# A rewritten order of work for a long convolution and a token MLP on one core: the same instructions, other queues' sequences

## The chip, the core and the metric

The program runs on one NeuronCore of a Trainium2 chip. The core has five engines with instruction queues of their own: PE (matrix multiply), ACT (ScalarE), DVE (VectorE), POOL (GpSimd) and SP, which here only issues DMA copies. Each queue runs in order. The metric is the device time of one execution in microseconds. The kernel before takes 170.63 us (median of three runs, 170.56 to 170.69).

## What is computed

Inputs are bf16; S = 2048 rows, D = 448 columns, F = 1792.

```python
def _A_ref(q, k, v, shift_k, ssm_k, ssm_D):      # q is already layer-normalized
    # k_shift: causal 4-tap convolution of k along S, one filter per column
    kv = k_shift * v
    # y: causal convolution of kv with ssm_k along S (2048 taps), by FFT of length 4096
    y = irfft(rfft(kv_pad) * rfft(kf_pad))[:S].astype(bf16)
    y = y + kv * ssm_D
    return q * y
def _B_ref(x, w1, b1, w2, b2):                   # x is already layer-normalized
    h = _layernorm(x)
    u = gelu(einsum("bsd,sf->bdf", h, w1) + b1)  # mixes the rows
    return (einsum("bdf,fs->bds", u, w2) + b2).transpose(0, 2, 1)
h  = x + _A_ref(_layernorm(x), ...)
h2 = h + _B_ref(_layernorm(h), ...)
```

## The kernel before

**How the work is staged.** Row s of a tensor lies in partition s // 16, at place s % 16; so one partition holds 16 rows. The long convolution is a transform in two stages of matmuls with sine tables, a product in the frequency domain, and two inverse stages. The code names its steps "tag.n:k": the n-th step of a tag, its k-th operation. The tags are:

- `loads`, `xload`: copies from memory: ssm_k (loads.0 to 3), shift_k (loads.4), k (loads.5, 6, 8, 10 for its slices 3, 0, 1, 2), v (loads.7, 9, 11, 12 for its slices 0, 1, 2, 3), ssm_D, the biases, and x in four slices (xload.0 to 3).
- `tables`: the sine tables and masks. `tables.5` and `tables.6` make the first-stage table E on DVE (integer phases, L837 to L844) and ACT (sine, L847). `tables.4` writes 16 small constants with GpSimd (L820, L821) and decodes the partition number on DVE, ending with a cast (L831, tables.4:20). `tables.7` makes the second-stage tables: three products on GpSimd that read the cast (L854), a sum (L858), a mask and two equality tests on DVE (L860, L866), a sine on ACT (L862) and three products and one negation on GpSimd (L871, L874).
- `kT`: transposes of ssm_k on PE (L1037) and their copies out of PSUM. `kv.1` to `kv.8`: transposes of k (L965). `kv.9` to `kv.16`: the 4-tap convolution as matmuls (L991); DVE multiplies the result with v (L1006).
- `k1`, `u1`: first stage for ssm_k and for k*v, 16 steps each (L1058), a copy out of PSUM (L1066, L1068), and after every second step three DMA copies (two from GpSimd's queue, one from SP's; L1074) that shuffle partitions.
- `k2`, `u2`: second stage (L1093) and copies out of PSUM (L738 to L742).
- `i1`: 16 products on DVE (L1160) in eight pairs, first inverse stage (L1177), copies out of PSUM, and DMA copies into TZ on SP's and GpSimd's queues (L1201; the last pair's, i1.16, L1188). Some of SP's copies fill only the last two of TZ's 16 rows.
- `ct0`, `ct`: transposes of E for the last stage (L1107). `ew`: small tables. `q`, `xn`: statistics of x on DVE (L1237, L1239) and GpSimd (L1245, L1248), and x normalized for four rows (L1270, L1272).
- `i2`: second inverse stage, one row of 16 per step (L1303, L1309), gate with q, layer norm of h; its last step writes a row of Q (L1388).
- `mlp.0` to `mlp.15`: the first MLP matmul for the first seven of 14 blocks of F, one row r each (L1435, W1A); `mlp.17` to `mlp.23`: the other seven blocks (L1445, W1B), with gelu on ACT (L1425); `mlp.24` to `mlp.39`: the second MLP matmul (L1457), the last sum on DVE (L1460) and the copies to the output. `w1a`, `w1b`, `w2`: the weights' copies (L1408, L1412, L1419). `warm`, `dummy`: matmuls whose result is not used. `bias`: a transpose of b1 and a cast of b2.

**What sets the order.** Nothing at run time. `ORDER` holds, for each engine, the whole sequence of its operations; `SLOTS` gives each PSUM tile its bank (eight banks; a tile of two banks takes a pair) and each shuffle buffer its place in a ring of four. The scheduler walks through these lists, checks dependences and emits each engine's instructions in the listed order, with the semaphore waits that the dependences need. So an operation that waits holds up whatever is listed behind it on its engine, and a DMA copy is issued when its queue's engine gets to it. Which of ACT and DVE empties a PSUM tile is also set by which list names it. Two dependences matter outside the data flow: the first product (i1.0) needs every shuffle copy of k1 and u1 to have landed, because its buffers lie in the same memory; and `w1a.1` to `w1a.3`, `w1b` wait for all of i1.16's copies:

```python
op(WQ, lambda e, W, rs=rs: e.dma_start(W1A[:, rs, :], w1d[:, rs, 0:896]),
   w=[(o_W1A + 4 * h * 1792, 4 * 1792)], dmab=128 * 4 * 1792,
   after=shuf["zl"] if h else shuf["u"], safter=(wl[0],) if h else ())
```

## Time and profile before

| | |
|---|---|
| median of three runs | 170.63 us |
| the profiled execution | 170.65 us, of it 168.8 us from the first to the last instruction |
| busy: PE, DVE, ACT, POOL | 160.0, 101.9, 90.4, 58.4 us |
| first product (L1160) starts, last ends | 49.91, 68.86 us |
| PE's first step that waits for i1.16's copies | 75.58 us |
| second MLP matmul | 123.86 to 165.94 us |

A line of the profile names the source line, the engine, the operation and the shapes. "Busy" adds up instructions; for PE the ends of matmuls are modelled, so a busy PE may still be waiting. "Idle before" is the time an engine stood still ahead of an instruction, with what ended it. The chain follows the work that ended last back through what released it. In a timeline the first number is the start, the second the length of a merged piece.

### The profile page before, as it was taken

To read this page: it belongs to the slowest core of one execution; us is meant where nothing else is said; L and a number is where in the kernel's file an instruction comes from. 1 tells how busy PE (TensorE), PEld (TensorE's weight loads), DVE (VectorE), ACT (ScalarE), POOL (GpSimd) and SP (SyncE) were. 2 spreads that over 40 slices of the span, in tenths; PEclk is the share of its full clock that TensorE was granted. 3 is DMA by queue.
4 is the path that set the end of the run, shared out by engine and by line. 5 is a ranking of instruction groups with operands and counts; after the bars stand their busy time and mean duration, and the time that the engine had idled before them with its cause. 6 is when DMAs were issued, how large, how long until landed. Compare 5 with 4: busy or idle time off the path is not lost.

```text
span 168.8 us, 3562 instructions
## 1 busy us (share of the span) xinstructions
PE 160.0 (95%) x1416; PEld 93.3 (55%) x1416; DVE 101.9 (60%) x191; ACT 90.4 (54%) x130; POOL 58.4 (35%) x155
## 2 busy tenths in 40 slices
PE   6999999989899989879999999999999999999994
PEld 2787755453333333334554555555577777777783
DVE  7988999999999999999987440000003213132231
ACT  3599848979999999999685803103550000000000
POOL 8345727694830555675777330000000000000000
DMA  5999898893758766748999999930000111101111
GB/s 161 407 308 385 270 290 327 329 362 126 222 134 318 248 195 186 208 135 273 388 398 403 424 420 422 415 129 0 0 0 9 50 54 54 54 2 56 54 54 54
DMA packets 15564, 35.15 MB, mean 208 GB/s; under 512 B 3804, under 2 KB 9644, under 8 KB 15548
## 3 DMA queue, kind: packets, MB, share of 16 engines
q1 hardware_dynamic: 12396, 28.26, 46.1%
q0 software_dynamic: 3008, 6.58, 12.1%
q8 instruction: 11, 0.18, 0.5%
q10 hardware_dynamic: 144, 0.08, 0.2%
q14 instruction: 5, 0.04, 0.1%
HBM read 22.05 MB, written 1.84 MB: 141 GB/s over the span
## 4 chain that ended last, share of the span: by engine, by line
PE 70%; ACT 14%; DMA 5%; DVE 5%; issue 2%; POOL 2%; SPq 0%; DVEq 0%; ACTq 0%
PE ps L1457 25%; PE ps L1435 13%; PE ps L1445 13%; ACT arena L738 7%; DMA arena<-arena 5%; ACT arena L739 4%; PE ps L1309 3%; PE ps L965 3%; ACT arena L1068 3%; PE ps L1024 3%; PE ps L1058 3%; PE ps L1037 3%; DVE arena L1160 2%; POOL arena L1074 2%; PE ps L991 2%
## 5 line engine op out<-in xcount | busy, mean ns | idle before, releaser
L1460 DVE SCALAR_TENSOR_TENSOR arena<-ps,arena 128x448 bf16<-128x448 f32 (+2 forms) x17 | 11.1, 656 | 55.8 <-PE ps L1457 55.8
L1457 PE MATMUL ps<-arena 128*128 128x448 bf16 (+2 forms) x238 | 42.7, 342 | 0.0
L1457 PEld LDWEIGHTS ps<-arena 128*128 128x128 bf16 x238 | 33.3, 145 | 9.5
L1435 PE MATMUL ps<-arena 128*128 128x448 bf16 x112 | 23.5, 353 | 0.0
L738 ACT CAST arena<-ps 128x896 bf16<-128x896 f32 (+1 forms) x29 | 23.1, 933 | 0.0
L1068 ACT CAST arena<-ps 128x896 bf16<-128x896 f32 x24 | 20.2, 919 | 4.1 <-PE ps L1058 3.6
L1445 PE MATMUL ps<-arena 128*128 128x448 bf16 x112 | 22.3, 352 | 0.0
L1074 POOL DMA_DIRECT2D arena<-arena x32 | 17.6, 556 | 7.9 <-ACT arena L1068 7.7
L1425 ACT ACTIVATE arena<-ps,arena 128x448 bf16<-128x448 f32 x14 | 8.2, 632 | 19.3 <-PE ps L1445 10.3
L1093 PE MATMUL ps<-arena 128*64 128x448 bf16 x128 | 15.3, 361 | 1.8 <-ACT arena L739 0.9
L1435 PEld LDWEIGHTS ps<-arena 128*128 128x128 bf16 x112 | 10.7, 98 | 10.6 <-DVE arena L1388 1.1
L1445 PEld LDWEIGHTS ps<-arena 128*128 128x128 bf16 x112 | 11.0, 98 | 10.2
L1160 DVE TENSOR_TENSOR arena<-arena 128x1792 bf16<-128x1792 bf16 x16 | 16.5, 1083 | 0.0
L1177 PE MATMUL ps<-arena 64*128 64x448 bf16 x128 | 14.1, 351 | 1.1 <-ACT arena L738 0.5
L1058 PE MATMUL ps<-arena 128*32 128x448 bf16 x256 | 14.5, 355 | 0.5 <-ACT arena L1068 0.3
L1201 POOL DMA_DIRECT2D arena<-arena x16 | 9.3, 585 | 13.9 <-ACT arena L738 13.0
L1093 PEld LDWEIGHTS ps<-arena 128*64 128x64 f16 x128 | 5.5, 108 | 10.7 <-ACT arena L739 3.4
L1177 PEld LDWEIGHTS ps<-arena 64*128 64x128 f16 x128 | 5.2, 94 | 9.8 <-DVE arena L1160 3.1
L1388 DVE TENSOR_SCALAR arena<-arena 128x448 bf16<-128x448 f32 x16 | 7.6, 509 | 4.8 <-POOL arena L1381 4.8
L1058 PEld LDWEIGHTS ps<-arena 128*32 128x32 f16 x256 | 5.2, 95 | 7.7 <-ACT arena L1068 2.6
L1237 DVE BATCH_NORM_STATS2 arena<-arena 128x6 f32<-128x448 bf16 x16 | 9.4, 613 | 0.0
L739 ACT ACTIVATE arena<-ps 128x896 bf16<-128x896 f32 x10 | 8.6, 926 | 1.1 <-PE ps L1093 1.1
(99 smaller groups left out, 190.4 us busy)
## 6 DMA issues: line engine op xcount, KB each, us to landing
arena<-in_B_w_dram SPq DMA_DIRECT2D x8, 896.0 KB, 9.9
arena<-in_B_w_dram SPq DMA_DIRECT2D x2, 2048.0 KB, 17.3
arena<-arena SPq DMA_DIRECT2D x16, 224.0 KB, 3.8
arena<-arena POOLq DMA_DIRECT2D x32, 112.0 KB, 3.6
arena<-in_B_w_dram SPq DMA_DIRECT2D x2, 1536.0 KB, 18.8
arena<-arena POOLq DMA_DIRECT2D x13, 196.0 KB, 3.8
arena<-in_A_k_dram SPq DMA_DIRECT2D x4, 448.0 KB, 5.8
arena<-in_A_v_dram SPq DMA_DIRECT2D x4, 448.0 KB, 9.2
```

Of the source, the lines that this page charges most:

```text
L738: return e.copy(out=dst(), in_=src())
L739: return e.activation(out=dst(), in_=src(), func=ACT.Copy, scale=scale)
L1058: op("pe", lambda e, W, b=b, r=r, q=q, x=x, c0=c0: e.matmul(PS[32 * q:32 * q + 32, b.slots[x], 0:D], E[:, 2 * r + x, c0:c0 + 32], src[:, r ...
L1068: return e.copy(out=dst, in_=Ppair(b)) if W == "act" else e.tensor_copy(out=dst, in_=Ppair(b))
L1074: shuf[tag].append(op(q_, lambda e, W, g=g, i=i, a=a, nu=nu, jh=jh: e.dma_start(T[a + i:a + i + 4 * nu - 3:4].rearrange("p (j k) c d -> p ...
L1093: op("pe", lambda e, W, b=bs[h], h=h, j=j, c=c, par=par: e.matmul(PS[64 * par:64 * par + 64, b.slots[c], 0:D], FW[:, 64 * c:64 * c + 64], ...
L1160: op("dve", lambda e, W, m=m, i=i: e.tensor_tensor(out=MR(m.slots[0]).rearrange("p (x y) d -> p x y d", x=2), in0=TU[:, i].unsqueeze(2).br ...
L1177: k = op("pe", lambda e, W, b=bs[h], m=ms[h], par=par, t=t, tab=tab, xy=xy, P=P: e.matmul(Pb(b, par), tab[P, :], MR(m.slots[0])[P, xy, :], ...
L1435: op("pe", lambda e, W, r=r, fc=fc, b=bs[fc]: e.matmul(Pb(b), W1A[:, r, 128 * fc:128 * fc + 128], Q[:, r, :], start=(r == 0), stop=(r == R ...
L1445: op("pe", lambda e, W, r=r, fc=fc, b=b: e.matmul(Pb(b), W1B[:, r, 128 * (fc - n0):128 * (fc - n0) + 128], Q[:, r, :], start=(r == 0), sto ...
L1457: op("pe", lambda e, W, r=r, fc=fc, b=b, d0=d0, d1=d1: e.matmul(Pb(b)[:, d0:d1], W2[fc // 7][:, fc % 7, r:S:R], G[:, fc, d0:d1], start=(fc ...
L1460: op("dve", lambda e, W, r=r, b=b, A=A, d0=d0, d1=d1: e.scalar_tensor_tensor(out=XR(r)[:, d0:d1], in0=Pb(b)[:, d0:d1], scalar=bm[:, r:r + ...
```

## The change

`ORDER` and `SLOTS` are written anew; every operation of before is there after it, none is added or taken away. On PE 1416 operations, on ACT 115, on DVE 177, on GpSimd 151 and on SP 79 stand in both. Thirteen PSUM copies, the small copy of bias.0 and one gate go from ACT to DVE and twelve copies, two gates and one normalization (xn.1) from DVE to ACT. The main moves:

- SP: ssm_k's slice 2 and k's slices 1 and 0 come first; xload.0 and xload.1 stand among the loads, ahead of v's; w1a.0 stands behind i1.16's copies; nine of the copies for TZ's last two rows (i1.1, 8, 10, 12, 14, 6) stand behind w1a.1, w1a.2 and w1a.3.
- GpSimd: the iotas for E come first; the constants of tables.4 are spread over the loads and the first stage; tables.7 stands among the shuffle copies of k1 and u1, and k1.1's first copy behind it.
- DVE: E's phases come first, tables.4:16 to 20 and tables.7 stand among the first-stage copies.
- ACT: E's sines come first, tables.7:5 behind u1.11.
- PE: kT.5 first, the 4-tap convolutions earlier between k1 and u1, ct0.0 behind u1.11, bias.0 behind i1.4, ct.0 behind i2.10, both warm-up matmuls ahead of i2.9; the MLP's matmuls are interleaved over rows and blocks.

The diff, cut ("-" before, "+" after):

```diff
 "pe":
-"dummy.0:1-9 kv.4:0-11 kv.3:0-7 kv.6:0-11 kv.5:0-7 kT.1:0-7 kT.0:0-3 kT.1:9-11 kT.0:4-7 kT.3:0-7 "
-"kT.2:0-3 kT.3:9-11 kT.5:0-7 kT.2:4-7 ct0.0:0-7 kT.6:0-7 kT.7:0-7 bias.0:0 kv.7:0-7 k1.8:0-7 k1.9:0-7 "
...
-"warm.0:0 i2.1:0-3 ct.1:0-7 i2.9:0-3 i2.2:0-1 i2.10:0-1 ct.2:0-7 i2.45:0-1 i2.17:0-1 i2.41:0-1 i2.20:0-1 "
-"i2.54:0-1 i2.28:0-1 i2.32:0-1 warm.1:0 mlp.0:2-6 i2.58:0-1 mlp.0:0-1 mlp.1:0-6 i2.67:0-1 mlp.2:0-6 "
...
+"dummy.0:1-9 kT.5:0-7 kv.6:0-11 kv.5:0-7 kT.4:0-7 kv.4:0-11 kv.3:0-7 kT.0:0-7 kT.1:0-7 kT.3:0-7 kT.1:9-11 "
+"kT.3:9-11 kT.6:0-7 kT.7:0-7 kv.2:0-11 kv.1:0-7 kv.7:0-7 k1.8:0-7 k1.10:0-7 k1.12:0-7 k1.9:0-7 kv.9:0-27 "
...
+"i1.16:10-17 i1.16:1-8 ct.2:0-7 ct.1:0-7 warm.0:0 warm.1:0 i2.9:0-3 i2.1:0-3 i2.2:0-1 i2.10:0-1 ct.0:0-7 "
+"i2.17:0-1 i2.45:0-1 i2.20:0-1 i2.32:0-1 i2.28:0-1 i2.54:0-1 i2.41:0-1 mlp.0:1 mlp.0:5 mlp.0:0 mlp.0:6 "
+"i2.58:0-1 mlp.1:1 mlp.1:5 mlp.0:2-3 mlp.1:2 mlp.1:0 mlp.0:4 mlp.1:4 i2.67:0-1 mlp.1:3 mlp.1:6 mlp.2:4 "
...
 "act":
-"tables.0:5 kv.4:12 kv.3:8 kv.6:12 tables.5:3 tables.6:3 ct0.0:8 bias.0:1 tables.7:5 k1.8:8 k1.9:8 "
...
+"tables.0:5 tables.5:3 kv.5:8 tables.6:3 kv.6:12 kT.3:8 kv.2:12 k1.8:8 k1.12:8 k1.10:8 k1.11:8 k1.13:8 "
+"kT.2:8 k1.14:8 k1.15:8 u1.0:8 u1.1:8 u1.2:8 k1.4:8 u1.3:8 k1.5:8 k1.6:8 k1.7:8 u1.4:8 u1.5:8 u1.8:8 u1.7:8 "
+"u1.10:8 u1.11:8 tables.7:5 u1.13:8 u1.14:8 k2.5:4 k2.1:4 u1.15:8 k2.9:4 k2.13:5 k2.7:4 k2.3:5 u2.13:4 "
...
 "dve":
-"dummy.0:0 tables.3:0-1 kv.0:3 tables.6:0 tables.4:16 tables.5:0 tables.4:17 tables.6:1 tables.4:18 "
-"tables.5:1 tables.4:19 tables.6:2 tables.4:20 tables.5:2 kT.1:8 tables.7:6 kT.0:8 kT.3:8 tables.7:4 "
...
-"q.3:3 u2.13:5 q.3:0 u2.1:5 i1.0:0 i1.1:0 i1.13:0 i1.14:0 i1.9:0 i1.7:0 i1.8:0 i1.10:0 i1.12:0 i1.11:0 "
-"i1.10:18 q.4:3 xn.0:1 i1.5:0 i1.6:0 i1.3:0 i1.6:9 xn.3:1 i1.2:0 i1.16:0 q.4:1 q.3:1 i1.15:0 q.6:0 q.6:2 "
...
+"dummy.0:0 tables.6:0 tables.3:0 tables.5:0 tables.6:1 tables.5:1 kv.0:3 tables.5:2 kT.5:8 tables.6:2 kT.4:8 "
+"tables.3:1 kT.0:8 kT.1:8 kv.3:8 kv.4:12 kT.6:8 kT.7:8 kv.0:4 kv.1:8 kv.7:8 q.1:2 k1.9:8 q.1:0 kv.9:29 "
+"kv.9:28 kv.13:28-29 kv.10:24-25 kv.12:25 kv.12:24 k1.0:8 kv.8:12 k1.1:8 kv.16:24 q.2:0 q.1:1 kv.16:25 q.2:2 "
+"kv.15:29 q.2:3 kv.15:28 tables.4:16-17 kv.11:29 kv.11:28 q.1:3 q.2:1 tables.4:18-19 kv.14:24 tables.4:20 "
+"kv.14:25 k1.2:8 u1.6:8 tables.7:6 u1.9:8 k1.3:8 tables.7:4 ct0.0:8 u1.12:8 q.4:2 q.3:0 k2.5:5 k2.1:5 "
+"tables.7:7 k2.9:5 k2.13:4 k2.7:5 k2.3:4 u2.13:5 u2.1:5 q.3:1 i1.0:0 k2.15:5 i1.14:0 i1.1:0 i1.13:0 i1.7:0 "
+"i1.9:0 i1.10:0 u2.11:5 i1.8:0 i1.12:0 i1.11:0 q.4:3 u2.5:5 q.6:2 i1.6:0 i1.5:0 xn.0:1 xn.3:1 i1.8:18 i1.3:0 "
+"i1.2:0 q.6:3 q.3:2 q.4:0 i1.16:0 i1.15:0 q.5:0 q.3:3 q.8:2 q.4:1 q.6:0 bias.0:1 q.6:1 q.5:1-2 q.7:0 q.5:3 "
...
 "pool":
-"tables.4:0 tables.4:2 tables.4:4 tables.4:6 tables.4:8 tables.4:10 tables.4:12 tables.4:14 tables.4:1 "
...
-"tables.2:7 tables.2:8 tables.2:9 tables.2:10 tables.2:11 tables.2:2 tables.2:4 tables.2:6 q.0:0 q.0:1 "
-"kv.0:1 kv.0:2 tables.7:0 tables.7:1 tables.7:2 tables.7:3 tables.7:8 tables.7:9 tables.7:10 tables.7:11 "
-"kv.0:0 k1.9:9 k1.9:10 k1.11:9 k1.11:10 k1.13:9 k1.13:10 k1.15:9 k1.15:10 u1.1:9 u1.1:10 k1.1:9 k1.1:10 "
...
+"tables.0:1-4 tables.0:0 tables.4:14 kv.0:2 kv.0:1 tables.4:13 tables.1:0 tables.4:12 tables.4:3 tables.4:1 "
...
+"tables.2:10 tables.4:9 k1.9:10 k1.11:10 k1.9:9 k1.15:9-10 k1.13:10 k1.1:10 tables.4:0 k1.13:9 u1.1:9 "
+"tables.2:0 u1.1:10 tables.4:6 tables.4:8 u1.3:10 u1.3:9 k1.5:9-10 q.0:0 tables.7:1-2 k1.7:10 k1.7:9 "
+"tables.7:0 tables.2:9 q.2:4 k1.1:9 tables.7:3 u1.9:9 k1.3:10 tables.7:8 k1.3:9 q.2:5 u1.13:10 u1.13:9 "
+"u1.5:10 u1.5:9 u1.9:10 u1.7:9 tables.7:9 u1.11:10 tables.7:10 u1.7:10 u1.15:9-10 u1.11:9 tables.7:11 ew.0:0 "
...
 "sp":
-"loads.6:0 loads.8:0 loads.0:0 loads.1:0 loads.2:0 loads.3:0 loads.13:1 loads.14:0 loads.14:1 loads.10:0 "
-"loads.5:0 loads.11:0 loads.4:0 loads.4:1 loads.4:2 loads.12:0 loads.9:0 loads.7:0 k1.9:11 k1.11:11 "
-"k1.13:11 k1.15:11 xload.0:0 xload.1:0 u1.1:11 k1.1:11 u1.3:11 k1.5:11 u1.5:11 k1.7:11 u1.7:11 u1.9:11 "
-"k1.3:11 u1.13:11 u1.11:11 u1.15:11 ct0.1:0 ct0.1:1 xload.2:0 xload.3:0 w1a.0:0 ct0.1:2 ct0.1:4 ct0.1:3 "
...
-"i1.4:18 i1.16:19 i1.16:20 w1a.1:0 w1a.2:0 w1a.3:0 w1b.0:0 w1b.0:1 w1b.0:2 w1b.0:3 w2.0:0 w2.0:1 w2.0:2 "
...
+"loads.2:0 loads.8:0 loads.6:0 loads.0:0 loads.1:0 loads.3:0 loads.4:2 loads.4:1 loads.5:0 loads.4:0 "
+"loads.10:0 xload.0:0 loads.11:0 loads.7:0 loads.12:0 loads.13:1 xload.1:0 loads.14:1 loads.9:0 k1.13:11 "
...
+"i1.10:22 i1.4:18 i1.16:19-20 w1a.0:0 w1a.1:0 i1.8:22 i1.8:20 w1a.2:0 i1.10:20 i1.1:20 i1.1:22 i1.12:22 "
+"i1.12:20 i1.14:20 w1a.3:0 i1.6:22 w1b.0:0-3 w2.0:0-3 mlp.25:15 mlp.27:15 mlp.29:15 mlp.31:15 mlp.33:15 "
...
```

`SLOTS` changes with it: the same tiles take other banks of the same eight.

136 rows, old and new, of tables (ORDER, SLOTS) are left out of this document.

## Prediction

> **What bounds the kernel now.** I read the page's totals and slices first, then the chain that ended last, then one table of the engines stage by stage, and only then single instructions.
>
> ```profile
> PE 160.0 (95%) x1416; PEld 93.3 (55%) x1416; DVE 101.9 (60%) x191; ACT 90.4 (54%) x130; POOL 58.4 (35%) x155
> ```
>
> PE at 95% would say that only matmul work counts. The table by stage (start:end, length, then busy time and count for PE, PEld, DVE, ACT, POOL, clock, DMA share, GB/s) says otherwise for the first half:
>
> ```profile
> 24.00:50.00 26.00, 23.84 (x372) 10.60 (x364) 25.22 (x39) 24.00 (x30) 16.79 (x34) 1.00 0.72 256
> 50.00:69.00 19.00, 17.68 (x160) 6.29 (x160) 18.75 (x24) 19.00 (x25) 7.60 (x13) 1.00 0.74 232
> 69.00:75.60 6.60, 5.10 (x46) 2.74 (x47) 6.25 (x17) 6.51 (x9) 5.29 (x9) 1.00 0.56 167
> 75.60:124.00 48.40, 48.40 (x255) 24.74 (x256) 19.23 (x57) 24.00 (x53) 14.91 (x39) 1.00 0.73 285
> ```
>
> From 24 to 69 us DVE is filled to 97% and 99%, ACT to 92% and 100%: they empty PSUM and make the products, and PE, busy by a model of its ends, waits for them. From 75.6 us PE is full (48.40 of 48.40). The chain, in order of time (start, length, what), joins the two:
>
> ```profile
> 67.89 0.99 DVE arena L1160
> 68.92 0.95 PE ps L1177 x8
> 69.89 0.91 ACT arena L738
> 70.82 0.67 SPq L1188
> 71.55 3.99 DMA arena<-arena
> 75.58 2.82 PE ps L1309 x14
> 123.86 42.08 PE ps L1457 x231
> ```
>
> So: the last of the 16 products on DVE (step i1.15) ends at 68.86; 6.7 us later its result has passed PE, ACT and a DMA copy, and the second half starts. That half has 90.4 us of PE work (75.58 to 165.94) without a gap. The change keeps every instruction, so it can gain only by an earlier last product, and lose by a later one or by a hole in the second half. The profiled execution took 170.65 us (span 168.8 and 1.85 around it) beside a median of 170.63, so I carry sums against either.
>
> How much idle time can DVE still give up before that last product? A table of DVE alone between its first instruction and 68.86:
>
> ```profile
> 0.89:68.86 67.97, 65.22 (x102) 1.00 0.81 269
> ```
>
> 2.75 us in all. That is the whole purse for a reordering that leaves DVE's work as it is.
>
> **The change part by part.** DVE's work ahead of the last product is not left as it is. Thirteen PSUM copies come to DVE and twelve go to ACT. In come ten of 128x896 (k1.9, u1.6, u1.9, k2.3, k2.5, k2.9, k2.15, u2.5, u2.11, i1.8) and three of 1024 (kv.3, kv.4, ct0.0), out go eight and four; one more statistics instruction (q.6) stands ahead of the product, one aggregate and a bias cast fewer. Prices, back to back (starts overlap by about 0.08 us):
>
> ```profile
> 43.44 3.10 DVE L742 TENSOR_SCALAR arena<-ps 128x896 bf16<-128x896 f32 x3
> 9.79 1.29 DVE L741 COPY arena<-ps 128x1024 bf16<-128x1024 bf16 x2 [0.19 <-PE ps L1037]
> 33.17 1.14 DVE L1237 BATCH_NORM_STATS2 arena<-arena 128x6 f32<-128x448 bf16 x2
> 49.91 10.22 DVE L1160 TENSOR_TENSOR arena<-arena 128x1792 bf16<-128x1792 bf16 x10
> ```
>
> That is 1.03, 0.64, 0.57 and 1.02 us. 2 x 1.03 - 0.64 + 0.57 - 0.17 = +1.8 us of DVE work. ACT's work to its last copy (i1.16) stays within 0.2 us. So DVE becomes the tighter of the two.
>
> Where it falls matters. Ahead of the first product (i1.0, at 49.91 before) the new order has 1.8 us less DVE work by the same prices: k2.15's second copy and two statistics now stand behind it. From the first product to the end of the last the old order takes 68.86 - 49.91 = 18.95 us; the new one puts four copies there (k2.15, u2.11, u2.5, i1.8) where two were (i1.10, i1.6), and three statistics (q.6, q.3, q.4) where none was: 2.06 + 1.7 - 0.1 = +3.65, so 22.6 us.
>
> Idle time on DVE before the first product, old, is 2.75 less about 0.25 behind it: 2.5 us. New, by place:
> - First instruction. GpSimd makes the two iotas that the first table product (L837) reads ahead of most memsets, so it can start near 1.7 instead of 2.2; DVE is idle 0.35 where it was 0.23.
>
> ```profile
> 1.55 0.34 DVE L810 TENSOR_SCALAR arena<-arena 128x128 bf16<-128x128 int32 x1 [0.23 <-POOL arena L789]
> 2.22 1.23 DVE L837 TENSOR_TENSOR arena<-arena 128x1024 int32<-128x1024 int32 x1
> ```
>
> - ssm_k chunk 2 is loaded first, chunk 0 fourth. DVE reaches kT.0's copy at about 9.2, PE has it transposed at about 9.8: 0.6; kT.6 and kT.7 some 0.4, k1.9 0.1.
> - Loads of x. Two xload slices of 448 KB move ahead of v's slices on SP's queue. The old v loads land up to 9.9 us after their issue at 9.8, so the last at 19.7; 0.92 MB at the 299 GB/s of the first 14 us put 3 us ahead of the last v slice, to about 22.5, and 1.2 us ahead of v's slice 0. DVE wants them at 17.9 (kv.9) and 21.4 (kv.12): a wait between 0 and 2; I take 0.6, since it arrives within a us of both.
> - Later evacuations (k1.1, kv.16) 0.3.
>
> ```profile
> 0.00:14.00 14.00, 12.63 (x132) 9.19 (x135) 12.29 (x26) 9.54 (x10) 7.22 (x47) 1.00 0.89 299
> L901 SPq DMA_DIRECT2D arena<-in_A_v_dram x4: 432/479/586, 6.4 to 9.8; - x4
> DMA to landing us min/median/max: 8.6/9.2/9.9
> ```
>
> - The tables, moved deep into the stretch. GpSimd's three table multiplications (L854) wait for a cast on DVE (L831). In the new order 27.5 us of DVE work stand between 1.7 us and that cast (six integer table steps, eleven transposed copies, fifteen products of L1006, and others by the rows shown), and some 2 us of idle: about 31.4. GpSimd is in order, so behind that wait stand the copies of k1.7, k1.1, u1.9, k1.3, u1.13, u1.5, u1.7, u1.11, u1.15. From the cast to the last copy's issue: 17 DMA issues of 0.54 (9.2), seven table instructions (2 x 0.36, 0.36, 1.0, 3 x 0.43), 1.1 of small ones: 13.7, so 45.1; it lands 2.4 to 3.7 later, 47.5 to 48.8. The first product needs all these copies (its buffers lie in theirs) and DVE gets to it at 48.1 or later: a wait between 0 and 0.7, I take 0.4. PE's first k2 step also waits for k1.1's copy (lands about 38) and for the FW table; PE, DVE and ACT have u1 copies to do until then.
>
> ```profile
> L1006 DVE TENSOR_TENSOR arena<-ps,arena 128x512 bf16<-128x512 f32 x12 | 7.7, 684 | 0.1
> L854 POOL TENSOR_SCALAR arena<-arena x3: 363/364/1331, 7.4 to 9.1; 128x128 int32<-128x128 int32 x3
> L1074 POOL DMA_DIRECT2D arena<-arena x32: 544/544/811, 16.6 to 45.5; - x32
> DMA to landing us min/median/max: 2.4/3.7/5.5
> 43.85 2.15 POOL L1074 DMA_DIRECT2D arena<-arena  x4 [0.36 <-ACT arena L1068]
> 9.53 1.02 POOL L858 TENSOR_TENSOR arena<-arena 128x384 int32<-128x384 int32 x1
> 14.29 1.29 POOL L871 TENSOR_TENSOR arena<-arena 128x128 f16<-128x128 f32 x3 [3.74 <-ACT arena L862]
> ```
>
> Together 2.75 us of idle instead of 2.5: +0.25. So the first product starts at 49.91 - 1.8 + 0.25 = 48.4, the last ends at 48.4 + 22.6 = 71.0, 2.1 us later than 68.86.
>
> Moved at no cost on PE: ct0.0's, ct.0's and bias.0's transposes (0.6 us for eight) lie where PE waits anyway. ct.0 now stands behind i2.10, so its copy on ACT must end before i2.45: in the old run i2.2 ran 2.4 us ahead of the copies' landing (73.21 against 75.58), enough for 0.6 of PE and 0.9 of ACT; without that cover it costs 0.9. A warm-up matmul moves ahead of the copies' landing; PE then waits those 0.2 us for the first normalized row (about 2.9 us behind the landing in both orders), so nothing.
>
> First weights (w1a.0) move from 50.2 us to just behind i1.16's copies. They are wanted 2.9 us behind the copies' landing; a slice took 4.7 us at the least, and this one is issued 3.3 before the landing (75.58 against 72.3), so it lands 1.4 behind it: hidden. Behind w1a.1, which waits for the landing, now queue nine small copies of TZ's last rows at 0.67 us on SP, 6.0 us with the 1.4 of the weight issues: SP gets through at 7.5 us behind the landing, the last copy lands 3.9 later (11.4). PE wants row 14 after 12 steps of i2 (0.38) and 40 matmuls of the MLP (0.19): 12.2. Covered by 0.8; were a landing 6.5, it would cost 1.8. I take 0.
>
> ```profile
> 73.21 0.92 PE L1309 MATMUL ps<-arena 128*128 128x448 bf16 x4 [0.22 <-issue]
> 73.96 0.61 PE L1107 MATMUL ps<-arena 128*128 128x128 f16 x8
> 75.58 2.82 PE L1309 MATMUL ps<-arena 128*128 128x448 bf16 x14 [1.01 <-DMA arena<-arena]
> 78.48 0.74 PE L1435 MATMUL ps<-arena 128*128 128x448 bf16 x3
> L1408 SPq DMA_DIRECT2D arena<-in_B_w_dram x4: 378/440/2027, 50.2 to 76.9; - x4
> DMA to landing us min/median/max: 4.7/7.1/8.6
> L1201 SPq DMA_DIRECT2D arena<-arena x12: 666/666/683, 55.1 to 69.1; - x12
> DMA to landing us min/median/max: 3.3/3.9/6.5
> ```
>
> The interleaved MLP order has the same matmuls in a stretch that is full already: 0. Sum: +2.1, so 172.8 us.
>
> **The rivals.**
> *Faster: DVE never waits.* The place is DVE ahead of the first product. With its 2.5 us of idle all gone, that product starts at 49.91 - 1.8 - 2.5 = 45.6 and the last ends at 68.2: -0.65, 170.0 us. For it: the sine tables come first on ACT, and ACT's 2.3 us wait at 21 to 23 us goes. Against: GpSimd's copies must land by 45.6 too, and the purse is all there is. It decides below 45.9 (0.34 us gained).
>
> ```profile
> ACT arena L1068 <- PE ps L1058: 3.6, 6, 2.3
> ```
>
> *No change:* first product at 45.9 to 46.6, 1.9 to 2.6 us of idle gone, 170.6.
> *Row 14 comes late:* with the last copies' landing at the slow end, 1.3 us more: 174.1. For it: weights fill the same queue; against: 0.8 us of cover.
> *GpSimd's tables stretch.* One L854 took 1331 ns and the two after it 363. The long one lay beside this DVE instruction, and ended with it:
>
> ```profile
> 7.20 1.23 DVE L844 TENSOR_SCALAR arena<-arena 128x2048 int32<-128x2048 int32 x1
> ```
>
> If each of the three took 1.33, the copies behind them would come 2.9 later and the first product at about 50.9: 175.2 us. In the new order PSUM copies run beside them instead, as beside the two short ones. The Trainium skill ("GPSIMD Engine Reference", section 1, Specifications) says GpSimd shares its SBUF interfaces with VectorE and is held up by two-port modes and by two SBUF inputs; by that rule the long one is such a case, the trace agrees, and the moved ones should be short.
> *A cold PE.* The first nine matmuls cost 0.39 us each (3.54), later ones of that size 0.19. If PE were as slow again after waiting for the TZ copies, nine matmuls' worth, 1.8 us, would be added: 174.6. The old run idled 1.01 there and went on at 0.2; the new one has about 1.9 us of wait.
>
> ```profile
> 1.37 3.54 PE L1024 MATMUL ps<-arena 128*128 128x448 bf16 x9 [1.37 <-DVE arena L1016]
> ```
>
> The Trainium skill ("TensorE: Matmul & The Clock Gate", Part 1) puts the gate's fall-back at an idle window of about 3.4 us; by that rule the wait stays short of it, and the old trace, where 1.01 us did nothing, does not contradict it.
>
> **How the numbers follow.** A measurement of this kernel tells about 0.2% (0.34 us) from no change. Chances: the forecast (171.3 to 173.7) 0.50; row 14 late 0.09; tables stretched 0.09; cold PE 0.05, together 0.73 slower; no change 0.12; DVE never waits 0.15. The range, 170.1 to 175.0, drops half of the fast case and the worst of the stretched one; the forecast's own range is 171.3 to 173.7, the ends of v's and the copies' waits.
>
> **What would show it.** The first product near 48.4 and 22.6 us from there to the last one's end near 71.0, DVE above 97% between; GpSimd waiting for L831 around 31 us with shuffle copies behind it; PE's first i2 step that waits for a landing near 77.7, and no PE gap behind it. Wrong if DVE's idle time before the first product is under 1 us, if the cast is done far earlier than 31 us, or if PE shows holes among the MLP's matmuls.

## The result and the profile after

The changed kernel takes 173.47 us (median of four runs, 173.39 to 173.86) beside 170.61 us of the kernel before on the same chip: a ratio of 1.0171, with a 95% interval of 1.0154 to 1.0189. The forecast of 172.8 us was 0.7 us low and inside its own range (171.3 to 173.7); its sign and its first half held, its second half did not. The profiled execution took 173.43 us (span 171.6). Ratios here and below are of fast runs; of all the executions told of, one was slow (176.38 us, of e1), and it stands in e1's median but not in its ratio.

Line numbers of the changed kernel are higher by nine for the same code: the products stand in L1169 (L1160 before), the waiting steps of i2 in L1318 (L1309), the second MLP matmul in L1466 (L1457). In the runs of the experiments they shift by a few lines more.

The table of the engines, cut this time at the kernel's own landmarks: DVE's first instruction, first product, end of the last product, first step that waits for i1.16's copies, first matmul of the second MLP layer. Columns: stretch, length, then busy time and count of PE, PEld, DVE, ACT, POOL, clock, DMA share, GB/s. The kernel before:

```profile
0.89:49.91 49.02, 46.38 (x724) 26.70 (x724) 46.52 (x79) 40.12 (x47) 30.21 (x87) 1.00 0.84 285
49.91:68.86 18.95, 17.68 (x160) 6.20 (x156) 18.70 (x25) 18.95 (x24) 7.60 (x13) 1.00 0.73 230
68.86:75.58 6.72, 5.17 (x45) 2.81 (x45) 6.37 (x17) 6.63 (x9) 5.29 (x9) 1.00 0.57 171
75.58:123.70 48.12, 48.12 (x254) 24.51 (x255) 19.25 (x58) 23.73 (x52) 14.91 (x39) 1.00 0.74 287
```

And the changed kernel:

```profile
0.89:48.76 47.87, 44.67 (x711) 25.72 (x711) 44.50 (x74) 38.85 (x44) 28.30 (x83) 1.00 0.84 290
48.76:70.77 22.01, 18.33 (x169) 7.14 (x169) 22.01 (x28) 21.12 (x26) 11.96 (x21) 1.00 0.52 151
70.77:77.11 6.34, 5.20 (x47) 2.95 (x47) 5.67 (x16) 5.25 (x7) 4.60 (x8) 1.00 0.73 214
77.11:126.48 49.37, 48.51 (x253) 23.93 (x254) 18.92 (x58) 23.10 (x51) 18.05 (x40) 1.00 0.79 298
```

Stage by stage the changed kernel is shorter by 1.15, longer by 3.06, shorter by 0.38, longer by 1.25: +2.78 of the +2.8 in span. Two readings matter. In the second row DVE is busy for 22.01 of 22.01 us: it sets that stretch. ACT, busy for 21.12, is less than a microsecond behind it. In the last row PE is no longer full: 48.51 of 49.37, where it was 48.12 of 48.12.

Where DVE stood still ahead of the last product, as one row for DVE alone and its two longest waits behind its first instruction (what waited, for whom: total, times, longest):

```profile
0.89:70.77 69.88, 66.51 (x102) 1.00 0.74 247
...
DVE arena L750 <- PE ps L1046: 1.6, 1, 1.6
...
DVE arena L1169 <- DMA arena<-arena: 0.8, 1, 0.8
```

The chain that ended last, some of its pieces in order of time (start, length, what):

```profile
2.60 7.95 DMA arena<-in_A_ssm_k_dram
11.31 1.14 PE ps L1033 x6
...
44.26 1.58 POOL arena L1083 x3
45.84 2.89 DMA arena<-arena
48.76 1.09 DVE arena L1169
...
67.95 1.74 ACT arena L747 x2
70.52 4.57 DMA arena<-arena
75.13 0.93 PE ps L1318 x4
76.56 0.88 issue
77.45 1.02 ACT arena L747
80.82 1.84 ACT arena L1328 x3
85.53 1.04 POOL arena L1390
```

Between 58.89 and 69.70 us the chain runs over ACT's copies, not over DVE's products, which shows how close the two are. Before, it went from the copies' landing (75.58) straight onto PE and stayed there. Now it leaves PE: ct.0's transposes stand behind two steps of i2 that wait for a copy that lands at 75.08, and from there it runs through the copies of ct.0 and ct.1 out of PSUM and the gates on ACT and through GpSimd's part of the layer norm. PE's timeline shows what that costs. Matmuls start 0.19 us apart, so a piece of two is followed after 0.38; here are three places where the next one came later:

```profile
83.11 0.54 PE L1444 MATMUL ps<-arena 128*128 128x448 bf16 x2
84.01 1.12 PE L1444 MATMUL ps<-arena 128*128 128x448 bf16 x5 [0.36 <-DVE arena L1397]
...
88.81 0.55 PE L1318 MATMUL ps<-arena 128*128 128x448 bf16 x2 [0.28 <-ACT arena L1328]
...
90.92 0.54 PE L1318 MATMUL ps<-arena 128*128 128x448 bf16 x2 [0.22 <-ACT arena L1328]
```

By starts the three are 0.52, 0.45 and 0.39 us, together 1.36. The stretch lost 1.25, for one warm-up matmul (about 0.2 us) that stood in it before stands ahead of it now, and there are smaller holes. L1397 writes a row of Q, L1328 is a gate.

### The profile page after: what moved, and what is told of

It reads as the page before. It is cut to its first block, busy times and chain, and to the rows that moved or that the text cites. A ratio compares the mean times of both kernels' runs of the same rounds, so it can differ in the third digit from the quotient of the medians.

```text
span 171.6 us, 3571 instructions
## 1 busy us (share of the span) xinstructions
PE 159.4 (93%) x1416; PEld 92.8 (54%) x1416; DVE 102.2 (60%) x191; ACT 90.8 (53%) x130; POOL 63.2 (37%) x155
## 4 chain that ended last, share of the span: by engine, by line
PE 58%; ACT 14%; DMA 11%; POOL 7%; DVE 5%; issue 3%; SPq 1%; DVEq 0%; ACTq 0%
PE ps L1466 25%; PE ps L1454 12%; PE ps L1444 9%; ACT arena L747 7%; DMA arena<-arena 7%; DMA arena<-in_A_ssm_k_dram 5%; PE ps L1067 4%; POOL arena L1083 4%; PE ps L1000 3%; DVE arena L1169 3%; ACT arena L1077 2%; ACT arena L1328 2%; PE ps L1046 1%; PE ps L1318 1%; PE ps L974 1%
## 5 line engine op out<-in xcount | busy, mean ns | idle before, releaser
L1466 PE MATMUL ps<-arena 128*128 128x448 bf16 (+2 forms) x238 | 42.7, 342 | 0.0
L1466 PEld LDWEIGHTS ps<-arena 128*128 128x128 bf16 x238 | 33.2, 145 | 9.6
L1444 PE MATMUL ps<-arena 128*128 128x448 bf16 x112 | 25.1, 353 | 0.4 <-DVE arena L1397 0.4
L1454 PE MATMUL ps<-arena 128*128 128x448 bf16 x112 | 23.8, 352 | 0.0
L747 ACT CAST arena<-ps 128x896 bf16<-128x896 f32 x27 | 22.8, 927 | 1.2 <-DVE arena L1169 0.5
L1077 ACT CAST arena<-ps 128x896 bf16<-128x896 f32 x24 | 20.4, 911 | 2.2 <-PE ps L1067 1.7
L1083 POOL DMA_DIRECT2D arena<-arena x32 | 17.9, 564 | 9.9 <-ACT arena L1077 9.8
L1169 DVE TENSOR_TENSOR arena<-arena 128x1792 bf16<-128x1792 bf16 x16 | 16.5, 1080 | 0.8 <-DMA arena<-arena 0.8
L1210 POOL DMA_DIRECT2D arena<-arena x16 | 9.6, 605 | 10.7 <-ACT arena L747 9.7
L1397 DVE TENSOR_SCALAR arena<-arena 128x448 bf16<-128x448 f32 x16 | 7.6, 509 | 4.0 <-POOL arena L1390 3.9
L747 ACT COPY arena<-ps 128x1024 bf16<-128x1024 bf16 (+1 forms) x8 | 7.9, 1010 | 3.0 <-PE ps L974 1.0
L1015 DVE TENSOR_TENSOR arena<-ps,arena 128x512 bf16<-128x512 f32 (+1 forms) x16 | 9.2, 612 | 0.1
```

The source lines that it names most:

```text
L747: return e.copy(out=dst(), in_=src())
L1077: return e.copy(out=dst, in_=Ppair(b)) if W == "act" else e.tensor_copy(out=dst, in_=Ppair(b))
L1083: shuf[tag].append(op(q_, lambda e, W, g=g, i=i, a=a, nu=nu, jh=jh: e.dma_start(T[a + i:a + i + 4 * nu - 3:4].rearrange("p (j k) c d -> p ...
L1169: op("dve", lambda e, W, m=m, i=i: e.tensor_tensor(out=MR(m.slots[0]).rearrange("p (x y) d -> p x y d", x=2), in0=TU[:, i].unsqueeze(2).br ...
L1210: op(q_, lambda e, W, j=j, p0=p0, a=a, b_=b_, j0=j0: e.dma_start(TZ[p0:p0 + 29:4, j0:j0 + (b_ - a) // 8].rearrange("p r c d -> p r (c d)") ...
L1444: op("pe", lambda e, W, r=r, fc=fc, b=bs[fc]: e.matmul(Pb(b), W1A[:, r, 128 * fc:128 * fc + 128], Q[:, r, :], start=(r == 0), stop=(r == R ...
```

## The experiments

Four stages suffice to compare all runs: the start of the first product, the length from there to the end of the last product, from there to the first step that waits for i1.16's copies, and from there to the second MLP layer. Times are medians, and the stages are those of one profiled execution each; the one of e5 and the one of e8 were the slowest of their six (177.37 and 175.23), that of e11 the fastest of its twelve (170.77). The kernel before took 170.43 to 170.77 us beside each group. An asterisk marks a profiled run in which PE's granted clock fell.

| kernel | us | first product | products | to landing | to second layer |
|---|---|---|---|---|---|
| before | 170.61 | 49.91 | 18.95 | 6.72 | 48.12 |
| changed | 173.47 | 48.76 | 22.01 | 6.34 | 49.37 |
| e1 | 174.93 | 48.47 | 21.26 | 7.57 | 50.55* |
| e2 | 172.32 | 50.36 | 20.62 | 6.13 | 48.11 |
| e3 | 172.91 | 48.43 | 22.01 | 6.89 | 48.70 |
| e4 | 172.44 | 50.26 | 18.96 | 6.23 | 50.23 |
| e5 | 176.55 | 49.23 | 22.88 | 7.95 | 50.38* |
| e6 | 175.05 | 48.69 | 21.97 | 7.15 | 50.18 |
| e7 | 173.40 | 48.56 | 22.00 | 5.90 | 49.80 |
| e8 | 174.25 | 49.09 | 22.00 | 7.74 | 49.45 |
| e9 | 176.41 | 47.67 | 22.00 | 6.80 | 52.78* |
| e10 | 173.89 | 48.66 | 22.01 | 6.54 | 49.53 |
| e11 | 171.42 | 49.64 | 18.95 | 7.12 | 48.11 |
| e12 | 174.57 | 48.45 | 22.02 | 7.66 | 49.51 |

The theory (A): DVE's work between the first and the last product sets the first half, and what the order puts there is paid in full. The rivals: (B) the small copies or another engine set it; (C) the second half.

**e2: the kernel before, with three statistics ahead of the last product.**

```diff
 "dve" of the kernel before, L1160 is i1.15
-"... i1.16:0 q.4:1 q.3:1 i1.15:0 q.6:0 q.6:2 q.5:0 ..."
+"... i1.16:0 q.4:1 q.3:1 q.6:0 q.6:2 q.5:0 i1.15:0 ..."
```

> The order before, with three statistics instructions (q.6, q.6, q.5) moved from behind the last product to right ahead of it. Theory A: the last product ends 1.6 us later, 70.5, the second half starts at 77.2, and the time rises by 1.6 to 172.2. Rival B: another engine or the copies were as late as DVE, and less than 0.5 shows: 170.6 to 171.1.

172.32 us, ratio 1.0088 (1.0053 to 1.0123). The table of the engines for e2, columns as above:

```profile
50.36:70.98 20.62, 17.69 (x160) 6.19 (x156) 20.37 (x28) 19.13 (x24) 8.20 (x14) 1.00 0.72 226
...
77.11:125.22 48.11, 48.11 (x253) 24.49 (x254) 19.41 (x58) 24.16 (x52) 14.94 (x39) 1.00 0.74 287
```

Three statistics of 0.56 us made the stretch 1.67 us longer, and the run 1.8 longer, where 1.6 was expected; the second half did not notice. (In the profile the first product came 0.45 us later than in the kernel before and the landing 0.59 sooner behind the last one; the two nearly cancel.) This is theory A in its plainest form.

**e1: the changed kernel, with three statistics and one aggregate behind the last product.**

```diff
 "dve" of the changed kernel: four operations moved
-"... u2.5:5 q.6:2 i1.6:0 ... i1.2:0 q.6:3 q.3:2 q.4:0 i1.16:0 i1.15:0 q.5:0 ..."
+"... u2.5:5 i1.6:0 ... i1.2:0 i1.16:0 i1.15:0 q.3:2 q.4:0 q.6:2 q.6:3 q.5:0 ..."
```

> The changed order, with three statistics instructions and one aggregate on DVE (q.6, q.3, q.4) moved from ahead of the last product to right behind it. Theory A (DVE's work ahead of the last product sets the start of the second half): that is 3 x 0.59 + 0.08 less the overlaps, 1.6 us; the last product ends near 69.1 instead of 70.77, TZ's copies land near 75.5 and the time falls by 1.6 to 171.9. Rival B (ACT or GpSimd holds the same stretch): the last product ends earlier, but ACT's last copy and the landing do not follow by more than 0.5; 173.0. Rival C (what was lost was lost in the second half): the landing comes earlier and the time stays at 173.4, since rows 4 to 7 are normalized later.

174.93 us (172.96 to 176.38), ratio 1.020 (1.0141 to 1.0258): slower than expected by 3 us. The table of the engines for its products, columns as above:

```profile
48.47:69.73 21.26, 18.07 (x169) 7.33 (x169) 20.53 (x24) 20.95 (x27) 11.36 (x20) 1.00 0.52 151
```

DVE had 1.48 us less to do there than in the changed kernel (20.53 for 22.01), but the stretch is only 0.75 us shorter, because DVE now waited 0.70 us for a copy of ACT's ahead of its last two products. The last product ended at 69.73, 1.04 us sooner where 1.6 was expected, and 0.29 of that is a sooner first product. So theory A holds in the changed kernel only down to the level of ACT.

The landing did not follow: it came 7.57 us behind the last product instead of 6.34, at 77.30. That is what rival B forecast, though ACT's last copy did come a microsecond sooner (71.66 instead of 72.71). The same copies were as slow in runs that left this stretch as it was (see the landing below), so one profile can't say whether this was chance. Then PE ran slowly. PE's timeline of e1:

```profile
74.71 0.93 PE L1324 MATMUL ps<-arena 128*128 128x448 bf16 x4 [1.09 <-DMA arena<-arena]
...
77.30 4.50 PE L1324 MATMUL ps<-arena 128*128 128x448 bf16 x14 [1.22 <-DMA arena<-arena]
```

The same 14 matmuls took 2.97 us in the changed kernel. PE alone, with the granted clock behind its busy time:

```profile
74.00:77.30 3.30, 1.38 (x12) 1.00 0.91 268
77.30:78.00 0.70, 0.70 (x2) 0.52 0.80 302
78.00:79.00 1.00, 1.00 (x4) 0.50 0.81 174
79.00:80.00 1.00, 1.00 (x4) 0.50 0.91 294
80.00:81.00 1.00, 1.00 (x5) 0.63 1.01 387
```

The clock fell to 0.50 for some 3.4 us: about 1.5 us lost. This was the prediction's rival of a cold PE; it did not occur in the changed kernel's own profile, and did here.

**e3 and e4: the two halves exchanged.** e3 has the changed order up to i1.16 and the order of before behind it, on all five engines; e4 the reverse. SP's queue is a special case: in e3 w1a.0 comes behind i1.16's copies, as in the changed kernel, and in e4 the whole queue is that of before, since all that the changed order puts behind i1.16 has been issued by then.

```diff
 e3, on each engine
-changed order behind i1.16:  "... i1.16:1-8 ct.2:0-7 ct.1:0-7 warm.0:0 warm.1:0 i2.9:0-3 ..."
+order of before:             "... i1.16:1-8 ct.0:0-7 warm.0:0 i2.1:0-3 ct.1:0-7 i2.9:0-3 ..."
```

> The changed order up to the last inverse stage (i1.16) on every engine, and from there the order before for all that is left. Theory A with a second term: the landing stays at 77.1 (+1.5 to the kernel before), the second half takes 48.3 us from there to the second MLP matmul as before, not 49.5, so 1.2 to 1.3 us come back: 172.2. Rival C (the holes in the second half come from the late start, not from its order): 173.4. Rival D (all was lost in the second half): 170.6.

> The order before up to the last inverse stage (i1.16) on every engine, and from there the changed order (SP had issued nearly all of the small TZ copies and the first weights by then, as before). Theory A with a second term: the landing stays at 75.5 and the second half takes 49.5 us instead of 48.3: 171.8. If the second half's order costs nothing by itself: 170.6.

172.91 us, ratio 1.0147 (1.0104 to 1.0191), and 172.44, ratio 1.0099 (1.0065 to 1.0133): each 0.6 to 0.7 us above what theory A expected, e3 even nearer to rival C's 173.4. The stages have to decide. The second half of e3 in the table of the engines, its one wait in PE's timeline, and its first row of Q in DVE's:

```profile
77.33:126.03 48.70, 48.10 (x254) 24.51 (x254) 19.18 (x57) 23.67 (x51) 14.88 (x39) 1.00 0.78 302
...
80.94 1.10 PE L1437 MATMUL ps<-arena 128*128 128x448 bf16 x5 [0.60 <-DVE arena L1323]
...
79.66 0.51 DVE L1390 TENSOR_SCALAR arena<-arena 128x448 bf16<-128x448 f32 x1
```

The second half of e4, and PE's waits in it (line, releaser: total, times, longest):

```profile
75.45:125.68 50.23, 48.77 (x252) 23.88 (x253) 19.29 (x58) 23.62 (x51) 18.17 (x40) 1.00 0.71 276
...
PE ps L1447 <- DVE arena L1400: 0.6, 2, 0.3
PE ps L1321 <- ACT arena L750: 0.5, 1, 0.5
PE ps L1321 <- ACT arena L1331: 0.3, 1, 0.3
```

With the order of before behind i1.16 the stretch is 48.1 us plus, in e3, one wait. The profile names a DVE instruction for it (L1323), but the row of Q that PE needs was written by 80.17. By the trace's record of landings w1a.0 came at 80.85, and PE went on at 80.94: it waited for the first weights. Without that wait nothing of rival C's late holes is left. With the changed order there the stretch is 50.2 us even when everything ahead of it, and all of SP's queue, is as before. So the loss of the second half belongs to the order of PE, ACT, DVE and GpSimd behind i1.16.

The two halves do not add up: 2.35 us by the changed front, 1.9 by the changed tail, 2.9 by both. In e3's profile 0.6 us is the wait for the first weights. In e3 and e4 the statistics are split between a front and a tail that were not made for each other; what that costs was not measured.

**e8, e9 and e12: where in the tail?** e8 takes TensorE's, ScalarE's and VectorE's tail from before, e9 GpSimd's and SyncE's. e12 makes two swaps in the changed kernel:

```diff
 e8, "dve" (likewise "pe" and "act"):
-"... i1.15:0 q.5:0 q.3:3 q.8:2 q.4:1 q.6:0 bias.0:1 q.6:1 ..."
+"... i1.15:0 bias.1:0 q.3:3 q.4:1 q.6:0 q.5:0 q.5:2-3 q.5:1 ..."
 e9, "pool" (likewise "sp"):
-"... i1.16:21-22 q.4:4 q.6:4 q.4:5 q.6:5 i1.6:20 i2.7:0 i2.15:0 i2.23:0-2 ..."
+"... i1.16:21-22 i1.6:20 i1.4:21 q.4:4 q.6:4 q.4:5 q.6:5 i2.7:0 i2.23:0-1 i2.15:0 i2.23:2 ..."
 e12, "act":
-"... xn.4:0 ct.0:8 ct.1:8 i2.46:0 ..."
+"... xn.4:0 ct.1:8 ct.0:8 i2.46:0 ..."
 e12, "dve":
-"... i2.5:0 i2.18:0 i2.6:0 i2.13:0 i2.21:0 ..."
+"... i2.5:0 i2.13:0 i2.6:0 i2.18:0 i2.21:0 ..."
```

> The changed kernel, with the order of TensorE, ScalarE and VectorE behind i1.16 as in the kernel before; GpSimd's and SyncE's order there stays the changed one. With all five engines so, the time was 172.91 and the stretch from the first waiting product of the second half to the first MLP product of the last layer 48.70. If the holes of the second half come from GpSimd's and SyncE's order (one small copy and the reciprocal of one block moved), the stretch stays at 49.2 to 49.4 and the time at 173.3 to 173.5; if they come from the order of the other three, the stretch is 48.6 to 48.8 and the time 172.8 to 173.0.

> The complement: the changed kernel, with only GpSimd's and SyncE's order behind i1.16 as in the kernel before. If those two make the holes, the stretch falls from 49.37 to 48.7 and the time to 172.8 to 173.0; if the other three make them, the stretch stays at 49.2 to 49.4 and the time at 173.3 to 173.5.

> The changed kernel with two swaps behind the last table product: ScalarE copies ct.1 (ready) ahead of ct.0 (for which it waits 0.97 us, to 76.54, in the changed kernel's trace), so that its first gate (i2.46) can start near 77.7 instead of 78.35; VectorE runs i2.13 and i2.6 ahead of i2.18, as in the kernel before, so that GpSimd's first operation of the second half (i2.7) starts near 78.2 instead of 78.87. Theory (these two orders make the holes of the second half): TensorE's waits of 0.5 us for the gates and 0.4 us for VectorE's L1397 go, the stretch from the first waiting product to the last layer's first product falls from 49.37 to 48.5 to 48.9 and the time to 172.6 to 173.0. Rival (the holes come from elsewhere, or move): the stretch stays at 49.2 to 49.5 and the time at 173.2 to 173.6.

e8: 174.25 us, ratio 1.0217 (1.0176 to 1.0257), stretch 49.45. e9: 176.41, ratio 1.0348 (1.0311 to 1.0386), stretch 52.78. e12: 174.57, ratio 1.0205 (1.0161 to 1.0249), stretch 49.51. None gained, and all three lie above every range that was expected for them. By e8 the loss would lie with GpSimd and SyncE; e9, which gives those two their old order, is worse, with one wait of 2.09 us for a row of Q and a clock of 0.50 behind it. Each mixture has waits that neither whole order has, so this pair settles nothing. In e12 both swaps worked locally (GpSimd's first operation of the second half came at 78.20, 0.12 behind the landing, instead of 1.8; ACT waited 0.15 for ct.0 instead of 0.97), and two of the holes stayed where they were, with a new one behind them. PE's timeline of e12:

```profile
84.73 1.12 PE L1450 MATMUL ps<-arena 128*128 128x448 bf16 x5 [0.34 <-DVE arena L1403]
...
89.60 0.55 PE L1324 MATMUL ps<-arena 128*128 128x448 bf16 x2 [0.35 <-ACT arena L1334]
...
94.67 0.55 PE L1450 MATMUL ps<-arena 128*128 128x448 bf16 x2 [0.38 <-DVE arena L1403]
```

Which of the tail's moves makes them stays open.

**e5: two copies off VectorE.**

```diff
 "dve": -"... q.4:3 u2.5:5 q.6:2 ... xn.3:1 i1.8:18 i1.3:0 ..."
 "act": +"... u2.5:4-5 ... u2.3:4 i1.8:18 i1.6:18 ..."
```

> The changed kernel with two evacuations ahead of the last table product (u2.5:5 and i1.8:18, 1.05 and 1.08 us on VectorE in its trace) given to ScalarE; nothing else moves. Theory A (VectorE's work ahead of the last product sets the first half): VectorE sheds 2.13 us, the last product ends near 68.8 instead of 70.77, the last small copies land near 75.3 to 75.6, and the time is 171.7 to 172.0, faster than the changed kernel by 1.4 to 1.8. Theory B (the queue of small copies behind the products sets the landing, as the run with the statistics put behind suggests): the last product ends near 68.8 all the same, but the copies still land at 76.5 to 77.1 and the time stays at 172.9 to 173.5.

176.55 us, ratio 1.0329 (1.0282 to 1.0376): both expectations missed, and the products took longer, 22.88 us. The table of the engines for that stretch:

```profile
49.23:72.11 22.88, 18.25 (x169) 7.09 (x169) 20.30 (x26) 22.40 (x28) 12.66 (x20) 1.00 0.49 144
```

DVE's waits from 48 to 72.5 us:

```profile
DVE arena L1174 <- ACT arena L752: 2.5, 2, 1.6
```

DVE's work fell by 1.7 us and ACT's rose to 22.40 of 22.88: now DVE's last products wait for ACT's copies. Both engines are nearly full there (in the changed kernel 22.01 and 21.12 of 22.01), so these copies could not be handed over; taking work out of the stretch helped, but only by half of it (e1). The rest of e5's loss is the landing (7.95 us) and another fall of the clock (the 14 matmuls took 4.30 us).

**e6 and e10: the front.** e6 makes the tables early again; e10 puts the six fillers on PE behind kT.7, so that kT.6 is not held up.

```diff
 e6, "dve":
-"... kv.15:28 tables.4:16-17 ... tables.4:18-19 kv.14:24 tables.4:20 ... tables.7:6 ... tables.7:4 ... tables.7:7 ..."
+"... tables.6:2 tables.4:16-20 kT.4:8 ... kv.4:12 tables.7:6 tables.7:4 tables.7:7 kT.6:8 ..."
 e10, "pe":
-"... kT.3:0-7 kT.1:9-11 kT.3:9-11 kT.6:0-7 kT.7:0-7 kv.2:0-11 ..."
+"... kT.3:0-7 kT.6:0-7 kT.7:0-7 kT.1:9-11 kT.3:9-11 kv.2:0-11 ..."
```

> The changed kernel with its table operations early again: on VectorE five constants (0.77 us together in its trace, at 29.2 to 32.0) behind tables.6, and three factors (0.91 us, at 34.3 to 41.8) behind kv.4, in ScalarE's and GpSimd's queues the other parts of the tables likewise ahead of the first shuffle copies. Theory A (VectorE's purse): 1.68 us of work goes into the wait of 1.64 us for kT.6, what follows 42 us on VectorE starts up to 1.6 us earlier, the last product ends at 69.2 to 70.0 and the time is 171.9 to 172.7. Theory B (something else pins the first product: the shuffle copies, landing at 48.74): VectorE gets to the first product sooner and waits there 1.5 to 2.4 us instead of 0.79; the first product stays near 48.7 and the time at 173.2 to 173.6.

> The changed kernel, with the six filler products (three of 0.35 us behind kT.1, three behind kT.3) put behind the transposes kT.7 on TensorE, so that kT.6 can start when its load lands (11.33) instead of at 12.38; VectorE's wait of 1.64 us for it falls to about 0.6. Theory A (VectorE's purse): what follows on VectorE starts 1.0 us earlier, the last product ends near 69.8 to 70.0 and the time is 172.5 to 172.8. Rival (other waits take its place, the second loads landing at 18.08 and 21.41 or the shuffle copies at 48.74): VectorE waits as much later, the last product stays at 70.5 to 70.9 and the time at 173.2 to 173.6.

e6: 175.05 us, ratio 1.0263 (1.0235 to 1.0291). e10: 173.89, ratio 1.0207 (1.0171 to 1.0243): both above every range that was expected. In both the first product stays at 48.7 us. The three longest of DVE's waits in e10, behind its first instruction and up to the first product:

```profile
DVE arena L1175 <- DMA arena<-arena: 0.7, 1, 0.7
DVE arena L756 <- PE ps L980: 0.7, 1, 0.7
DVE arena L756 <- PE ps L1052: 0.5, 1, 0.5
```

The wait for kT.6 fell from 1.6 to 0.5 and a new one of 0.7 stood behind the fillers' new place; of 1.1 us won, 0.1 was left at the first product. In e6 1.7 us of tables went into the hole for kT.6, and the waits came back, most of them between 29 and 43 us. DVE's waits in e6:

```profile
DVE arena L1076 <- PE ps L1068: 0.6, 2, 0.5
DVE arena L1016 <- PE ps L1001: 0.5, 2, 0.3
DVE arena L1078 <- DMA arena<-arena: 0.5, 1, 0.5
```

So neither run could spend DVE's idle time ahead of the first product. In e10, as in the eight other runs whose front is the changed kernel's, that product starts 0.02 or 0.03 us behind the landing of the last shuffle copy (48.64): the copies hold it. In e6 that copy landed at 48.44 and DVE itself came 0.25 us later; the wait at the first product that theory B had there is gone.

What holds the copies is only argued, from the chain above: it goes back over PE, the tables and copies in GpSimd's queue, to the load of ssm_k. In e9, whose front is the changed kernel's, that load (loads.1) landed at 9.46 instead of 10.55 us and the first product came at 47.67 instead of 48.76. But in e3 the two were 9.91 and 48.43, in e5 10.53 and 49.23, so the load is not all of it.

e6's time is worse than its front: the landing and the second half took 0.8 us each. In the second half PE waited 1.34 us for one step of i2, and went on at 92.43, right behind the landing of row 14's last copy (92.34). This is the prediction's rival of a late row 14, in the size that it gave.

**e7 and e11: SyncE's queue alone.** e7 gives the changed kernel the old place of w1a.0 and of the nine copies for rows 14 and 15; e11 gives the kernel before the new places.

```diff
 e7, "sp" of the changed kernel:
-"... xload.3:0 ct0.1:4 i1.14:22 ct0.1:2-3 ... i1.16:19-20 w1a.0:0 w1a.1:0 i1.8:22 i1.8:20 w1a.2:0 ..."
+"... xload.3:0 w1a.0:0 ct0.1:4 i1.14:22 i1.14:20 ct0.1:2-3 ct0.1:5 i1.1:20 i1.1:22 ... i1.16:19-20 w1a.1:0 w1a.2:0 ..."
 e11, "sp" of the kernel before:
-"... xload.3:0 w1a.0:0 ct0.1:2 ... i1.1:20 i1.1:22 i1.14:20 i1.14:22 ... i1.16:19-20 w1a.1:0 w1a.2:0 w1a.3:0 ..."
+"... xload.3:0 ct0.1:2 ... i1.14:22 i1.10:22 i1.4:18 i1.16:19-20 w1a.0:0 w1a.1:0 i1.8:22 i1.8:20 w1a.2:0 i1.10:20 ..."
```

> The changed kernel with SyncE's queue as in the kernel before: the first weights (w1a.0) ahead of the small copies, and the nine copies of rows 14 and 15 as soon as they are evacuated. The prediction priced both moves at nothing: the time stays at 173.3 to 173.6. Rival: nine more copies in front of the last ones cost them the 0.4 us by which the changed kernel's copies land sooner behind their evacuation (4.36 against 4.74 us), but row 14's wait of 0.2 to 0.3 us near 91 goes: 173.5 to 173.9.

> The kernel before, with SyncE's queue behind the inverse copies as in the changed kernel: w1a.0 behind i1.16, and the nine copies of rows 14 and 15 between the first weights; everything else as before. The prediction priced both at nothing: 170.4 to 170.8. Rival 1 (the queue of small copies is what follows the last product): the copies of i1.16 land 0.4 to 1.0 us sooner than 4.74 us behind their evacuation and the time is 169.6 to 170.2, better than both kernels. Rival 2 (rows 14 and 15 or the first weights come late): the first MLP products or i2.93 wait, 171.0 to 172.5.

e7: 173.40 us, ratio 1.0167 (1.0144 to 1.0190), no different from the changed kernel, as expected. e11: 171.42, ratio 1.0041 (1.0023 to 1.0060), above what was expected and inside the range of its second rival. The second half of its profiled execution is untouched, with w1a.0 and the rows 14 and 15 late, in the table of the engines:

```profile
75.71:123.82 48.11, 48.11 (x253) 24.49 (x254) 19.00 (x57) 23.68 (x51) 14.93 (x39) 1.00 0.81 304
```

So in this execution the moves cost the second half nothing, as priced. But it was the fastest of twelve; the 0.6 us of the median is not in the trace, and the second rival's waits are not excluded.

Other traces show that the price is not always nothing. With w1a.0 behind i1.16's copies, the first MLP matmul started right behind the first row of Q in the changed kernel, e11 and e12. In e3, e6, e8, e9 and e10 it started 0.3 to 1.6 us behind that row and 0.09 to 0.14 us behind the landing of w1a.0. e10 is the worst: the row was written at 79.77, w1a.0 landed at 81.26, and PE, which had waited 1.36 us, went on at 81.39. The holes of the changed kernel behind it are then all but gone, but the stretch is no shorter (49.53).

No experiment points to an order that beats the kernel before, so none was tried.

## Why the prediction was right, and where it was not

- *DVE bounds the first half:* shown, by 22.01 of 22.01 and by e2; in the changed kernel ACT is so close behind that e1 got back only 0.75 us for 1.48.
- *DVE's work ahead of the last product, +1.8 us:* 66.51 - 65.22 = +1.29. Ahead of the first product 44.50 - 46.52 = -2.02 (priced -1.8); behind it +3.31 of work (priced +3.75).
- *First product at 48.4:* 48.76. Idle time ahead of it 3.37 us, priced at 2.75. The list of places was wrong one by one: kT.6 took 1.64 for 0.4, the copies 0.79 for 0.4, but kT.0 and v's loads nothing for 0.6 each. PE reached kT.0 in time, and v's slices 0 and 1 landed at 18.08 and 21.41 without a wait on DVE.
- *22.6 us from there, last end at 71.0:* 22.01, and 70.77. The first product came 0.36 late and the term was 0.59 too long: two errors that partly cancel.
- *The purse of idle time:* the prediction let it be spent or not (chance 0.15). e6 and e10 did not spend it: first products at 48.69 and 48.66 us, though e6 put 1.7 us of work into the hole and e10 took 1.1 us of wait away.
- *The tables on GpSimd:* the cast stood at 31.91 (31.4), the last shuffle copy was issued at 45.84 (45.1) and landed at 48.74, the end of the range given. They were not stretched (0.38 to 0.44 us each, where a stretched one took 1.33), as the rule weighed there from the Trainium skill ("GPSIMD Engine Reference", section 1) has it. The wait for the cast is there, in GpSimd's timeline of the changed kernel:

```profile
32.18 0.73 POOL L863 TENSOR_SCALAR arena<-arena 128x128 int32<-128x128 int32 x2 [0.43 <-DVE arena L840]
...
34.03 0.44 POOL L863 TENSOR_SCALAR arena<-arena 128x128 int32<-128x128 int32 x1
```

- *Landing near 77.7:* 77.11, with 6.34 us behind the last product instead of 6.72. Runs with the same copies in the same order took 6.34 to 7.74 (changed, e3, e6, e8 to e10, e12; one profile each), and with the order of before 6.13 to 6.72 (before, e2, e4), so the 0.38 can't be put down to the change. In the profiles, e12's time beside the changed kernel's (+1.1) is the landing's (7.66 against 6.34).
- *The first weights:* w1a.0 landed at 79.73, the MLP began at 80.05. Hidden, by 0.3 us; it was put 1.4 behind the landing and came 2.6, for the copy took 5.6 us from issue to landing where the working took the least, 4.7. Other runs with it in this place took 6.2 to 7.5, and in five of the nine it was not hidden (e3, e6, e8 to e10). That it cost nothing in the changed kernel's profile is in part luck.
- *Row 14:* its last copy landed at 90.83, 13.7 us behind the landing where 11.4 was priced: it took 6.6 us, the slow end that the rival named, and not 3.9. PE wanted it at about 90.5, later than priced, because of the holes ahead of it. A part of the last hole of 0.39 us is its: in e7, with these copies early, that hole is 0.20. In e6 the same copy cost 1.3 us.
- *"The interleaved MLP order has the same matmuls in a stretch that is full already: 0":* this is the step that failed, and with it ct.0's "nothing". It measured +1.25 us (e4: +2.1). A stretch that is full has no slack: its matmuls can be as many as before, and still one that comes up before ACT's gate or DVE's row of Q is ready makes a hole that nothing fills. The working priced what PE does there, and the order of ACT, DVE and GpSimd, by which the rows become ready, not at all. The prediction did name holes among the MLP's matmuls as a sign of being wrong, and they came.
- *A cold PE, 1.8 us:* not in the changed kernel; 1.5 us in e1 and much the same in e5 and e9. Where it came, the size was about right.

So 2.1 + 0 was forecast, and 1.53 + 1.25 came. The direction came from the right cause, DVE's work among the products. That the total came within 0.7 us is in part luck: the first half was put 0.6 us too high and the second 1.25 too low.

## What to carry to other kernels

Ask of each stretch not only how much idle time an engine has but what holds the end of the stretch. Idle time ahead of a point that copies hold was not gained by edits ahead of it (e10, where the copies still came last; in e6 the engine itself then came last, by 0.25 us), while work pushed behind that point, into a stretch where the engine is full, was paid in full (e2: 1.68 us of work, 1.67 us of time). Taking it out again gains only down to the next engine's level (e1: 1.48 and 0.75). A full engine is a reason to look at who feeds it: a new order of its inputs had nothing to gain there, and lost whatever it made late.

Compare stage by stage: the totals of e1 and e12 hold a late landing, e1's a slow clock as well, and say little of what their edits did. And don't take the named releaser of a wait on trust: in e3 and e10 it was a DVE instruction, and the landing of a copy stood behind it.
